# Layer two keeps squared h in SBUF, splits x later, and issues its odd bf16 products in eight tiles

## The chip, the cores and the metric

One core of a Trainium2 chip runs the whole program. The metric is device time in microseconds (us) of that core, as the median of several executions. The core's engines appear under these names: PE is TensorE (matmul), PEld its weight loads, DVE is VectorE, ACT is ScalarE, POOL is GpSimd, and SP is the queue from which all transfers are issued.

## The reference

```python
def _attn_ref(q, k, v) -> np.ndarray:
    B, H, S, D = q.shape
    factor = 4
    ...
    q_d = q.reshape(B, H, Sd, factor, D).mean(axis=3)
    ...
    out_up = np.repeat(out_d, factor, axis=2)
    pos = np.arange(S)
    mask = np.abs(pos[:, None] - pos[None, :]) < factor
    scores = scale * np.matmul(q, k.transpose(0, 1, 3, 2))
    scores = np.where(mask, scores, -1000000000.0)
    ...
    return (out_up + out_local).astype(np.float32)

def _moe_ref(x, w_in, w_out) -> np.ndarray:
    h = x @ w_in
    r = np.maximum(h, 0.0)
    g = r * r
    return (g @ w_out).astype(np.float32)
...
    x = np.ascontiguousarray(attn_out.transpose(0, 2, 1, 3)).reshape(B * S, H * D)
    x = _moe_ref(x=x, **moe_kwargs)
    return _moe2_ref(x=x, **moe2_kwargs)
```

q, k and v have 4 batches of 8 heads, 576 positions and 64 columns, so x is 2304 tokens by 512; both layers go from 512 to 2048 columns and back, and `_moe2_ref` computes the same as `_moe_ref` with its own weights. All is fp32.

## The kernel before

**Tiling.** The 2304 tokens are nine tiles of 256. The loop of the matmuls goes over 18 tiles, `n` = 0 to 8 for layer one and 9 to 17 for layer two (`NT` = 9), and in each over eight blocks of 256 hidden columns, `p` = 0 to 7. One pair (n, p) is a step. Attention and the conversion of the weights run between the steps of layer one.

**Precision by parts.** Each fp32 operand is kept as a high part (rounded by an fp32r cast) and a low part (operand minus high part), and a product of two operands is three products: high by high, high by low, low by high. x is split by `split_x` (line 841): two ACT casts of 512 columns give `xH`, two subtractions give `xL`, on DVE or POOL, whichever is planned to be free earlier (`either`, line 385). `fetch` (line 832) loads the x of a layer-two tile; `make_room` leaves one buffer `xr` for it.

**A step of layer two.** `mm_h` (line 863) makes h in one PSUM bank with 24 products of 256 columns. `act_h` (line 884) then works on ACT: Relu and Square in place in PSUM, a copy of the 128 columns a21 into the tile `S`, the cast of h to the high part of g, and, when the sums in `S` are there, their cast `SH`. `low_g` (line 909) works on DVE: four sums of 128 columns (the operand sums of a seven-product block scheme of Strassen's kind), the low part of g (h minus its high part), and the low part of the sums, `gSL`. `mm_y2` (line 936) issues 21 products: 12 that use the sums and 9 that use g alone. So a step is 45 products, against 48 in layer one, and PE runs h(i+1) between h(i) and y(i). In the first step of a tile (`p` = 0) the nine products on g come first, since the others wait until the tile before has left its accumulators.

**The end of a tile.** `leave` (line 1033) copies one quarter from PSUM on ACT and makes seven sums of 256 columns on DVE (line 1066) into a staging tile `ld[0]` or `ld[1]`, which is then stored.

**From layer one to layer two.** `quarters` (line 777) prepares differences of the second layer's output weights. `reload` (line 809) loads each 1024-column weight again from DRAM when layer one has done with it, rounds it on ACT and makes its low part on DVE or POOL. The last reloads, of `p` = 6 and 7, run beside the first steps of tile 9.

**The order.** Every chain above is a generator, and `Order.run` (line 136) is a list scheduler: at each turn it takes the operation that could start earliest by a model of durations, and writes the engines' queues in that order. An engine runs its queue strictly in order. A kind `DVP` in this plan is a DVE operation that also reserves the port which POOL shares with DVE (`PORT`, line 125).

**Odd products.** For steps listed in `KICK` (line 47), `mm_h` first issues one 128-column bf16 product of two identity matrices into the h bank (line 870); the next product overwrites it.

Of the kernel before, what the change touches and what calls it, by code (L numbers as in the profile page):

```python
# [8 lines left out]
F32 = mybir.dt.float32  # L9
# [13 lines left out]
NT = B * S // TN  # L23
# [20 lines left out]
NEAR = 0.02  # L44
FG = 0.4
FT = 3
KICK = {(n, 1) for n in (10, 12, 14)}
CL, GL, HL = 4, 4, 6
CP, CD, GP, UP = -0.848, 0.436, -1.416, -1.019
QP, VP, HP = -0.537, 0.649, -0.76  # L50
# [9 lines left out]
class Order:  # L60
# [75 lines left out]
    def run(self):  # L136
        while True:
            self.poll()
            best = None
            for th in self.live:  # L140
                if th.wish is not None and not callable(th.wish):
                    some = th.wish if isinstance(th.wish, list) else [th.wish]
                    _, t, eng, dur, *rows = min((self.start(th, w[0]) + w[1] * BIAS.get(w[0], 1.0), self.start(th, w[0]), *w) for w in some)
                    key = t
                    if best is None or key < best[0] - NEAR:
                        best = key, t, th, eng, dur, rows
            if best is None:
                assert not self.live, "nothing can start"
                return
            _, t, th, eng, dur, rows = best  # L150
            if eng in ("DVP", "POOL"):
                self.free["PORT"] = t + dur
            eng = "DVE" if eng == "DVP" else eng
            self.eng = eng
            if eng == "PE":
                if self.fill:
                    now = max(self.free.get("PE", 0.0), FT)
                    while now + FG < t:
                        now = self.stream(now, 0.22, 1.0)
                        self.fill()  # L160
                dur = self.stream(t, dur, *rows) - t
            if eng == "SP":
                self.free[eng] = t + (rows[0] if rows else 0.46)
                self.free["DMA"] = max(t + 1.1, self.free.get("DMA", 0.0)) + dur
                value = self.free["DMA"] + 2.0
            else:
                self.free[eng] = t + dur
                value = t + dur + LATENCY[eng]
            th.last, th.done = eng, value - LATENCY[eng]
            self.resume(th, value)  # L170
# [46 lines left out]
def attention_two_mlp_kernel(  # L217
# [151 lines left out]
    def dve(cols):  # L369
        return "DVE", 0.065 + cols / 957.0  # L370
# [11 lines left out]
    def act(cols):  # L382
        return "ACT", 0.065 + cols / 1150.0

    def either(cols):
        return [dvp(cols), pool(cols)]
# [390 lines left out]
    def quarters():  # L777
        yield lambda: ev.get("room")
        for p in range(NP):
# [19 lines left out]
            f_ld.put(n, tt)  # L799
            ev["T", p] = tt  # L800

    def quarter(p, name, low):
        if name in ("T3", "T4", "T2"):
            w, c = place[p, low][("T3", "T4", "T2").index(name)]
            return w[:, c:c + 256]
        m = ("B11", "T1", "B21", "B22").index(name)
        return weight(p, 1, low, 2)[:, m // 2, m % 2 * 256:m % 2 * 256 + 256]

    def reload(p, kind):
        yield o.at("scr", p, kind)  # L810
        if kind == 0:
            yield o.at("h", NT - 1, p)
        else:
            yield o.at("y", NT - 1, p)

        hi = weight(p, kind, 0, 2).rearrange("p k f -> p (k f)")
        some = pieces(p, kind, 1, 2, 0, 1024)
        for lo, c, n1 in some:
            yield dma(128 * 4 * n1, 4096 if n1 == 1024 else 2048)
            nc.sync.dma_start(out=lo.bitcast(F32), in_=wscr[p][kind][:, c:c + n1])  # L820
        for lo, c, n1 in some:
            yield act(n1)
            evac(hi[:, c:c + n1], lo.bitcast(F32))
        for lo, c, n1 in some:
            tt = yield either(n1)
            engine().tensor_tensor(out=lo, in0=lo.bitcast(F32), in1=hi[:, c:c + n1].bitcast(F32), op=ALU.subtract)
        count(("w", 2, p), 2, tt)

# [12 lines left out]
    def split_x():  # L841
        for n, (layer, t) in enumerate(seq):
            yield o.at("x", n)
            if n >= NXL:
                yield o.at("h", n - NXL, NP - 1)
            i = x_buf[n]
            for c in range(2):
                ks = slice(2 * c, 2 * c + 2)
                yield act(512)
                evac(xH[n % NXL][:, ks], xr[i][:, ks])  # L850
            for c in range(2):
                ks = slice(2 * c, 2 * c + 2)
                tt = yield either(512)
                engine().tensor_tensor(  # L854
                    out=xL[n % NXL][:, ks], in0=xr[i][:, ks], in1=xH[n % NXL][:, ks].bitcast(F32), op=ALU.subtract
                )
            f_xr.put(i, tt)
            ev["split", n] = tt
# [25 lines left out]
    def act_h():  # L884
        for i, st in enumerate(steps):
            yield o.at("h", *st)
            h = hb[i % 2]
            yield act(512)
            nc.scalar.activation(out=h, in_=h, func=AF.Relu)  # L889
            yield act(512)  # L890
            nc.scalar.activation(out=h, in_=h, func=AF.Square)  # L891
            if seq[st[0]][0] == 2:
                yield lambda: ev.get("room")
                if seq[steps[i - 1][0]][0] == 2:
                    yield o.at("gl", i - 1)
                if i == last:
                    yield o.at("y", *steps[i - 2])
                ev["sq", i] = yield act(128)
                nc.scalar.copy(late2["S"][:, 0:128], h[:, 128:256])
            ev["gh", i] = yield act(512)  # L900
            nc.scalar.copy(g_of(i, 0), h)  # L901
            if seq[st[0]][0] == 2:
                yield o.at("S", i)
                if seq[steps[i - 1][0]][0] == 2:
                    yield o.at("yS", i - 1)
                ev["gsh", i] = yield act(512)
                nc.scalar.copy(late2["SH"], late2["S"])  # L907

    def low_g():
        for i, st in enumerate(steps):  # L910
            two = seq[st[0]][0] == 2
            h = hb[i % 2]
            if two:


                yield o.at("sq", i)
                a11, _, a12, a22 = (h[:, 128 * m:128 * m + 128] for m in range(4))
                s1, s2, s3, s4 = (late2["S"][:, 128 * m:128 * m + 128] for m in range(4))
                for dst, a, b, op in (
                    (s3, a11, s1, ALU.subtract), (s1, s1, a22, ALU.add), (s2, s1, a11, ALU.subtract),  # L920
                    (s4, a12, s2, ALU.subtract),
                ):
                    tt = yield dve(128)
                    nc.vector.tensor_tensor(out=dst, in0=a, in1=b, op=op)  # L924
                ev["S", i] = tt
            yield o.at("gh", i)
            tt = yield dve(512)
            nc.vector.tensor_tensor(out=g_of(i, 1), in0=h, in1=g_of(i, 0).bitcast(F32), op=ALU.subtract)  # L928
            ev["gla", i] = tt
            if two:  # L930
                yield o.at("gsh", i)
# [238 lines left out]
```

## Time and profile before

| | us |
|---|---|
| median of 3 runs | 916.38 |
| lowest and highest run | 911.27, 916.97 |
| the profiled execution | 915.1 |
| its span, first to last instruction | 913.3 |
| mean granted TensorE clock, share of full speed | 0.988 |

The profile is that of one execution; its span leaves out 1.8 us of the time. A PE that is shown busy is not PE at its peak, since matmuls overlap: a stretch is best judged by the distance between the starts of equal work, such as one step to the next. Idle time is put down to the instruction that released the engine.

### The profile page before, as it was taken

The page shows a single profiled execution, that of the slowest core. Times are in us where ns is not written, and L with a number is a line of the kernel's source. Part 1 is how long each engine was busy: PE and PEld are TensorE (multiplying, and loading weights), DVE is VectorE, ACT ScalarE, POOL GpSimd, SP SyncE. Part 2 cuts the span into 40 slices and gives each one's busy share as a digit, 9 for nine tenths or more (in the row PEclk, how much of TensorE's full clock was granted, in tenths as well). Part 3 has the DMA queues.
Part 4 walks back from the last instruction along what each step waited for, and adds up shares of the span by engine and source line. Part 5 has one row for each costly group of instructions (what it writes and reads, how often), then busy time and mean ns, then how long its engine had stood idle before and what let it go on. Part 6 is the DMA issues. An engine that isn't in the chain of part 4 may idle for free.

```text
span 913.3 us, 20806 instructions
## 1 busy us (share of the span) xinstructions
PE 894.6 (98%) x8696; PEld 859.1 (94%) x8696; DVE 496.0 (54%) x1016; ACT 524.6 (57%) x1030; POOL 72.6 (8%) x78
## 2 busy tenths in 40 slices
PE   9989999999999999999999999999999999999996
PEld 5579999999999999999999989999999999999996
DVE  5696863575873534233324564655555564645454
ACT  3798974565577665543436655455545455545443
POOL 4211200020300000000001010000000000000000
PEclk9789999999999999999999999999999999999999
DMA  9999921363466676321216520101011010100000
GB/s 182 243 238 243 217 67 38 110 163 74 115 191 210 191 235 207 129 82 36 84 43 214 193 92 2 47 2 47 2 47 48 1 48 1 47 1 24 1 24 24
DMA packets 92430, 90.48 MB, mean 99 GB/s; under 512 B 62256, under 2 KB 68272, under 8 KB 92336
## 3 DMA queue, kind: packets, MB, share of 16 engines
q1 hardware_dynamic: 92336, 89.15, 35.6%
q8 instruction: 68, 1.11, 0.5%
q14 instruction: 26, 0.21, 0.1%
HBM read 70.25 MB, written 18.87 MB: 98 GB/s over the span
## 4 chain that ended last, share of the span: by engine, by line
PE 83%; DVE 5%; DMA 4%; ACT 4%; issue 1%; SPq 1%; POOL 0%; ACTq 0%; POOLq 0%
PE h L877 39%; PE y L961 18%; PE at L944 12%; PE y L944 4%; PE at L961 3%; DMA s<-in_moe_w_out_dram 2%; DVE S L924 1%; PE at L452 1%; DVE ld L1066 1%; DMA ld<-in_v_dram 1%; PE at L643 1%; DMA s<-in_moe_w_in_dram 1%; DVE xL L854 1%; PE at L588 1%; PE at L478 1%
## 5 line engine op out<-in xcount | busy, mean ns | idle before, releaser
L877 PE MATMUL h<-xH,w 128*128 128x256 f32 x2304 | 317.2, 281 | 1.7 <-ACT xH L392 1.7
L877 PEld LDWEIGHTS h<-xH,w 128*128 128x128 f32 x2304 | 287.4, 189 | 4.2 <-ACT xH L392 1.8
L961 PE MATMUL y<-g,w 128*128 128x256 f32 x1536 | 191.0, 279 | 0.7 <-ACT g L901 0.6
L889 ACT ACTIVATE h<-h 128x512 f32<-128x512 f32 x144 | 84.0, 583 | 179.2 <-PE h L877 179.0
L961 PEld LDWEIGHTS y<-g,w 128*128 128x128 f32 x1536 | 180.7, 188 | 3.6 <-ACT g L901 1.8
L877 PE MATMUL h<-xL,w 128*128 128x256 f32 x1152 | 180.4, 279 | 2.1 <-DVE xL L854 2.1
L928 DVE TENSOR_TENSOR g<-h,g 128x512 fp32r<-128x512 f32 x144 | 98.6, 685 | 115.7 <-ACT g L901 113.5
L877 PEld LDWEIGHTS h<-xL,w 128*128 128x128 f32 x1152 | 154.3, 189 | 2.6 <-DVE xL L854 2.6
L924 DVE TENSOR_TENSOR S<-h,S 128x128 f32<-128x128 f32 x144 | 41.9, 291 | 158.0 <-ACT g L901 152.8
L907 ACT CAST SH<-S 128x512 fp32r<-128x512 f32 x72 | 44.8, 622 | 97.4 <-DVE S L924 93.8
L891 ACT ACTIVATE h<-h 128x512 f32<-128x512 f32 x144 | 84.2, 585 | 3.4
L901 ACT CAST g<-h 128x512 fp32r<-128x512 f32 x144 | 84.9, 589 | 1.4
L854 POOL TENSOR_TENSOR xL<-xr,xH 128x512 fp32r<-128x512 f32 x14 | 19.7, 1405 | 478.7 <-ACT xH L392 478.7
L933 DVE TENSOR_TENSOR gSL<-S,SH 128x512 fp32r<-128x512 f32 x72 | 51.1, 710 | 10.0 <-ACT SH L907 1.1
L944 PE MATMUL at<-w,SH 128*128 128x256 f32 x224 | 45.4, 284 | 1.9 <-ACT SH L907 1.9
L924 DVE TENSOR_TENSOR S<-S,h 128x128 f32<-128x128 f32 x144 | 41.4, 288 | 5.6 <-ACT g L901 0.8
L944 PEld LDWEIGHTS at<-w,SH 128*128 128x128 f32 x224 | 34.1, 189 | 3.3 <-ACT SH L907 2.7
L944 PE MATMUL at<-w,g 128*128 128x256 f32 x240 | 35.0, 282 | 0.4 <-DVE g L928 0.4
L944 PE MATMUL at<-w,gSL 128*128 128x256 f32 x112 | 32.4, 289 | 1.4 <-DVE gSL L933 1.3
L944 PEld LDWEIGHTS at<-w,g 128*128 128x128 f32 x240 | 31.3, 192 | 0.6 <-DVE g L928 0.6
L459 DVE TENSOR_REDUCE qkd<-at 128x256 f32<-128x1024 f32 (+1 forms) x19 | 20.9, 1108 | 12.6 <-ACT qkT L392 12.5
L392 ACT ACTIVATE qkT<-at 128x1024 f32<-128x1024 f32 (+1 forms) x19 | 17.8, 936 | 16.9 <-PE at L452 16.7
(248 smaller groups left out, 1207.8 us busy)
## 6 DMA issues: line engine op xcount, KB each, us to landing
s<-in_moe_w_in_dram SPq DMA_DIRECT2D x32, 256.0 KB
s<-in_moe_w_out_dram SPq DMA_DIRECT2D x16, 512.0 KB
ws<-ga SPq DMA_DIRECT2D x32, 256.0 KB
w<-ws SPq DMA_DIRECT2D x13, 512.0 KB
ld<-in_moe_w_in_dram SPq DMA_DIRECT2D x12, 512.0 KB
ld<-in_moe_w_out_dram SPq DMA_DIRECT2D x10, 512.0 KB
xr<-ys SPq DMA_DIRECT2D x9, 512.0 KB
vw<-in_v_dram SPq DMA_DIRECT2D x68, 64.0 KB
```

The lines of the kernel that those rows point to most:

```text
L459: nc.vector.tensor_reduce(out=qkd[:, :, :, 32 * c:32 * c + n // 4], in_=got.rearrange("p z m (g r) -> p z m g r", r=4), op=ALU.add, axis=AX.X,
L854: engine().tensor_tensor(out=xL[n % NXL][:, ks], in0=xr[i][:, ks], in1=xH[n % NXL][:, ks].bitcast(F32), op=ALU.subtract)
L877: nc.tensor.matmul(out=o, lhsT=wt[p, 0][:, 1084:1340][:, fs] if w is wL and kk == 0 and p in ODD else w[:, kk, fs], rhs=x[:, kk], start=(i ...
L889: nc.scalar.activation(out=h, in_=h, func=AF.Relu)
L891: nc.scalar.activation(out=h, in_=h, func=AF.Square)
L901: nc.scalar.copy(g_of(i, 0), h)
L907: nc.scalar.copy(late2["SH"], late2["S"])
L924: nc.vector.tensor_tensor(out=dst, in0=a, in1=b, op=op)
L928: nc.vector.tensor_tensor(out=g_of(i, 1), in0=h, in1=g_of(i, 0).bitcast(F32), op=ALU.subtract)
L933: nc.vector.tensor_tensor(out=late2["SL"], in0=late2["S"], in1=late2["SH"].bitcast(F32), op=ALU.subtract)
L944: nc.tensor.matmul(out=seven(n, m - 1), lhsT=lhsT, rhs=quarter(p, w, low), start=p == 0 and x == 0 and m not in (2, 3, 6), stop=p == NP - ...
L961: nc.tensor.matmul(out=yb[e // 2][:, (e % 2) * 256:(e % 2) * 256 + 256], lhsT=w[:, fi, e * 128:e * 128 + 128], rhs=g[:, fi * 256:fi * 256 ...
```

## The change

- **h squared goes to SBUF.** The staging tile `ld[1]` is given up after the last `quarters` and serves as two halves of 512 columns, `late2["G"]`. In layer two, Relu reads PSUM and writes G, Square works in place in G, and the cast to g, the four sums and the low part of g read G. The copy of a21 into `S` is gone, and so is the wait for the step before that it had. The sums and the low part are planned as `DVP`.
- **The next tile's x.** In layer two both `xL` subtractions are on DVE. From the first step of layer two on, the scheduler adds 1.2 us to the key of a `split_x` operation, so that one is chosen only where nothing else can start within 1.2 us.
- **Reload.** The weights of `p` = 6 and 7 come in pieces of 256 columns (16 in place of 5 pieces), with their low parts on DVE alone.
- **Odd products.** They stand in the fourth step of the eight tiles 10 to 17, where they stood in the second step of tiles 10, 12 and 14.

```diff
 NEAR = 0.02
 FG = 0.4
 FT = 3
-KICK = {(n, 1) for n in (10, 12, 14)}
+LAZY = dict(split_x=1.2)
+FINE, HALF = 6, 1
+KICK = {(n, 3) for n in range(10, 18)}
 CL, GL, HL = 4, 4, 6
 CP, CD, GP, UP = -0.848, 0.436, -1.416, -1.019
 QP, VP, HP = -0.537, 0.649, -0.76
...
                 if th.wish is not None and not callable(th.wish):
                     some = th.wish if isinstance(th.wish, list) else [th.wish]
                     _, t, eng, dur, *rows = min((self.start(th, w[0]) + w[1] * BIAS.get(w[0], 1.0), self.start(th, w[0]), *w) for w in some)
-                    key = t
+
+                    key = t + (LAZY.get(th.gen.__name__, 0.0) if ("h", NT, 0) in self.ev else 0.0)
                     if best is None or key < best[0] - NEAR:
                         best = key, t, th, eng, dur, rows
             if best is None:
...
             f_ld.put(n, tt)
             ev["T", p] = tt
 
+        yield from f_ld.give_up([1])
+        late2["G"] = [ld[1].bitcast(F32)[:, 512 * m:512 * m + 512] for m in range(2)]
+        ev["G"] = 0.0
+
     def quarter(p, name, low):
         if name in ("T3", "T4", "T2"):
             w, c = place[p, low][("T3", "T4", "T2").index(name)]
...
 
         hi = weight(p, kind, 0, 2).rearrange("p k f -> p (k f)")
         some = pieces(p, kind, 1, 2, 0, 1024)
+        if p >= FINE:
+            some = [(x[:, u:u + 256 * HALF], c + u, 256 * HALF) for x, c, n1 in some for u in range(0, n1, 256 * HALF)]
         for lo, c, n1 in some:
             yield dma(128 * 4 * n1, 4096 if n1 == 1024 else 2048)
             nc.sync.dma_start(out=lo.bitcast(F32), in_=wscr[p][kind][:, c:c + n1])
...
             yield act(n1)
             evac(hi[:, c:c + n1], lo.bitcast(F32))
         for lo, c, n1 in some:
-            tt = yield either(n1)
+            tt = yield either(n1) if p < FINE else dvp(n1)
             engine().tensor_tensor(out=lo, in0=lo.bitcast(F32), in1=hi[:, c:c + n1].bitcast(F32), op=ALU.subtract)
         count(("w", 2, p), 2, tt)
 
...
                 evac(xH[n % NXL][:, ks], xr[i][:, ks])
             for c in range(2):
                 ks = slice(2 * c, 2 * c + 2)
-                tt = yield either(512)
+                tt = yield either(512) if layer == 1 else dvp(512)
                 engine().tensor_tensor(
                     out=xL[n % NXL][:, ks], in0=xr[i][:, ks], in1=xH[n % NXL][:, ks].bitcast(F32), op=ALU.subtract
                 )
...
         for i, st in enumerate(steps):
             yield o.at("h", *st)
             h = hb[i % 2]
-            yield act(512)
-            nc.scalar.activation(out=h, in_=h, func=AF.Relu)
-            yield act(512)
-            nc.scalar.activation(out=h, in_=h, func=AF.Square)
-            if seq[st[0]][0] == 2:
-                yield lambda: ev.get("room")
-                if seq[steps[i - 1][0]][0] == 2:
-                    yield o.at("gl", i - 1)
+            two = seq[st[0]][0] == 2
+            if two:
+                yield lambda: ev.get("G")
                 if i == last:
                     yield o.at("y", *steps[i - 2])
-                ev["sq", i] = yield act(128)
-                nc.scalar.copy(late2["S"][:, 0:128], h[:, 128:256])
+            g = late2["G"][i % 2] if two else h
+            ev["relu", i] = yield act(512)
+            nc.scalar.activation(out=g, in_=h, func=AF.Relu)
+            ev["sq", i] = yield act(512)
+            nc.scalar.activation(out=g, in_=g, func=AF.Square)
             ev["gh", i] = yield act(512)
-            nc.scalar.copy(g_of(i, 0), h)
+            nc.scalar.copy(g_of(i, 0), g)
             if seq[st[0]][0] == 2:
                 yield o.at("S", i)
                 if seq[steps[i - 1][0]][0] == 2:
...
 
 
                 yield o.at("sq", i)
-                a11, _, a12, a22 = (h[:, 128 * m:128 * m + 128] for m in range(4))
+                a11, a21, a12, a22 = (late2["G"][i % 2][:, 128 * m:128 * m + 128] for m in range(4))
                 s1, s2, s3, s4 = (late2["S"][:, 128 * m:128 * m + 128] for m in range(4))
                 for dst, a, b, op in (
-                    (s3, a11, s1, ALU.subtract), (s1, s1, a22, ALU.add), (s2, s1, a11, ALU.subtract),
+                    (s3, a11, a21, ALU.subtract), (s1, a21, a22, ALU.add), (s2, s1, a11, ALU.subtract),
                     (s4, a12, s2, ALU.subtract),
                 ):
-                    tt = yield dve(128)
+                    tt = yield dvp(128)
                     nc.vector.tensor_tensor(out=dst, in0=a, in1=b, op=op)
                 ev["S", i] = tt
             yield o.at("gh", i)
-            tt = yield dve(512)
-            nc.vector.tensor_tensor(out=g_of(i, 1), in0=h, in1=g_of(i, 0).bitcast(F32), op=ALU.subtract)
+            g = late2["G"][i % 2] if two else h
+            tt = yield dvp(512) if two else dve(512)
+            nc.vector.tensor_tensor(out=g_of(i, 1), in0=g, in1=g_of(i, 0).bitcast(F32), op=ALU.subtract)
             ev["gla", i] = tt
             if two:
                 yield o.at("gsh", i)
```

## Rows read from the trace of the kernel before

**Rows 1.** The page: PE's busy time and share; granted clock in 40 equal slices.
```profile
PE 894.6 (98%) x8696; PEld 859.1 (94%) x8696; DVE 496.0 (54%) x1016; ACT 524.6 (57%) x1030; POOL 72.6 (8%) x78
PEclk9789999999999999999999999999999999999999
```

**Rows 2.** Chain that ended last, 570 to 700: start, length, engine, tile, line, products.
```profile
582.05 2.83 PE h L877 x24
...
650.95 2.83 PE h L877 x24
653.78 2.47 PE at L944 x21
656.33 2.79 PE h L877 x24
...
661.49 2.72 PE h L877 x24
...
671.89 2.72 PE h L877 x24
...
687.22 2.72 PE h L877 x24
```

**Rows 3.** Timeline of PE (start, length, instruction): first and last products of layer two.
```profile
519.84 0.40 PE L877 MATMUL h<-xH,w 128*128 128x256 f32 x2
...
906.46 0.28 PE L944 MATMUL at<-w,gSL 128*128 128x256 f32 x1
```

**Rows 4.** Timeline of PE, h(9,2) to h(9,3); in brackets idle time and releaser.
```profile
530.40 0.28 PE L877 MATMUL h<-xH,w 128*128 128x256 f32 x1
...
535.16 0.51 PE L944 MATMUL at<-w,SH 128*128 128x256 f32 x2 [1.88 <-ACT SH L907]
...
539.76 0.51 PE L877 MATMUL h<-xH,w 128*128 128x256 f32 x3
```

**Rows 5.** Busy time of a stretch; last three: granted clock, DMA share, GB/s.
```profile
519.84:541.00 21.16, 19.06 (x151) 18.66 (x150) 14.50 (x26) 13.51 (x25) 2.41 (x1) 0.92 0.43 150
```

**Rows 6.** Timelines of ACT and DVE in the same stretch.
```profile
534.49 0.62 ACT L907 CAST SH<-S 128x512 fp32r<-128x512 f32 x1 [2.07 <-DVE S L924]
...
532.66 1.22 DVE L826 TENSOR_TENSOR w<-w 128x1024 fp32r<-128x1024 f32 x1
```

**Rows 7.** Timeline of PE, tile borders, first and last of six.
```profile
573.32 0.84 PE L944 MATMUL y<-w,g 128*128 128x256 f32 x6
...
581.89 0.28 PE L877 MATMUL h<-xH,w 128*128 128x256 f32 x1
...
825.83 0.28 PE L944 MATMUL y<-w,g 128*128 128x256 f32 x1
...
834.40 0.28 PE L877 MATMUL h<-xH,w 128*128 128x256 f32 x1
```

**Rows 8.** Timelines of POOL and DVE at the border of tiles 13 and 14.
```profile
743.45 1.30 POOL L854 TENSOR_TENSOR xL<-xr,xH 128x512 fp32r<-128x512 f32 x1 [40.76 <-ACT xH L392]
...
743.50 1.79 DVE L854 TENSOR_TENSOR xL<-xr,xH 128x512 fp32r<-128x512 f32 x1
```

**Rows 9.** Timelines of ACT and DVE, an ordinary step.
```profile
711.45 0.58 ACT L889 ACTIVATE h<-h 128x512 f32<-128x512 f32 x1 [1.77 <-PE h L877]
...
713.47 0.29 DVE L924 TENSOR_TENSOR S<-h,S 128x128 f32<-128x128 f32 x1 [3.07 <-ACT g L901]
...
715.47 0.69 DVE L933 TENSOR_TENSOR gSL<-S,SH 128x512 fp32r<-128x512 f32 x1
```

**Rows 10.** Groups by line and shape: count, busy us, mean ns of one, idle before.
```profile
L907 ACT CAST SH<-S 128x512 fp32r<-128x512 f32 x69 | 42.9, 622 | 93.5 <-DVE S L924 91.4 <-PE at L944 2.1
...
L1041 ACT COPY ld<-y 128x512 f32<-128x512 f32 x4 | 2.1, 586 | 2.7 <-PE y L961 2.7
...
L392 ACT ACTIVATE w<-w 128x256 fp32r<-128x256 f32 x3 | 1.2, 407 | 0.0
```

**Rows 11.** One line's instructions (last of `quarters`): shortest/median/longest ns, first and last start.
```profile
L796 DVE TENSOR_TENSOR q_hd<-ld,q_hd x1: 421/421/421, 496.5 to 496.5; 128x256 fp32r<-128x256 f32 x1
```

## The prediction

> **What bounds it now.** I read the page first. PE is busy for 98% of the span and its clock is granted in full except in the first slices and around the change of layers [rows 1]. So what can be won is time in which PE waits, or in which its products stand further apart than they could. The change touches layer two and the last reloads before it, so layer two is what I take apart, by the chain of waits and PE's timeline.
>
> The chain shows two distances. A step (45 products) takes 15.33 / 3 = 5.11 us in the stretch from 671.89, but 68.90 / 13 = 5.30 us from 582.05 [rows 2]. The engine is as busy in both, and the clock is granted in full in both slices. So the same products run at 113.6 or at 117.8 ns each, and a spacing once entered lasts. A slow step costs 0.19 us.
>
> The products of layer two start at 519.84 and the last one starts at 906.46 [rows 3], 386.6 us later. At the fast distance, 72 steps and the last y block of layer one, which stands among them (24 products, 2.7), would need 368.0 + 2.7 = 370.7 us. The excess is 16.0 us (rounded), and the timeline of PE divides it:
>
> - The change of layers: from 530.40 to 539.76 PE makes one step in 9.36 us, 4.25 too many [rows 4].
> - Six of the eight tile borders: y, h, y (66 products, 7.5 us when fast) take 8.57 us at the first and at the last of them [rows 7]; the six lose between 0.2 and 1.1 us each, 5.3 in all.
> - Slow distance behind two of these borders: from 582.05 until the odd product ahead of 656.33 [rows 2], 14 steps, and from 834.40 [rows 7] through the last h, some 12 steps: 26 x 0.19 = 5.0.
> - Three odd products. The h block behind one starts 0.08 us late (653.78 + 2.47 = 656.25, and it starts at 656.33), and the step that it opens takes 5.16 in place of 5.11 [rows 2]: 0.13 each, 0.4.
> - What is left, 1.05, lies in the last three y blocks.
>
> **The change, part by part.**
>
> *h squared in SBUF.* In an ordinary step Relu starts at 711.45, the first sum on DVE at 713.47, and gSL ends at 715.47 + 0.69 = 716.16: 4.71 us [rows 9]. PE needs it one step after h, 5.11, so there are only some tenths of slack. The first sum reads h and the copied a21, both long there, yet the row puts its wait on the cast of g, which also only reads h. That cast stands in the way of the sums. The Trainium skill has a reason (PSUM — Partial Sum Buffer, section on bank collisions): no two engines may access one PSUM bank at once, two reads included, so software keeps them apart. The trace agrees: 2.02 us from Relu to the first sum. After the change the bank is read by Relu alone, and the sums need only Square. Relu from PSUM to SBUF I take as the copy of y, 586 ns, Square and the cast from SBUF to SBUF as the cast SH, 622 ns [rows 10]. The first sum then starts 0.59 + 0.62 + 0.07 (two hand-overs) = 1.28 after Relu, 0.74 earlier; four sums and SH follow unchanged, and gSL ends about 4.0 after Relu, 0.7 earlier. The sums and the low part with both inputs in SBUF I price as now; gSL, 0.69, has such inputs already. If the sums still stand behind the cast, the first one starts at 1.28 + 0.62 = 1.9 and the gain is 0.1: these are the two ends, and I take 0.7, because of the named releaser.
>
> A rule of the skill speaks against this part (VectorE: DVE Perf Modes, the section on the TRN2 errata): a ScalarE operation costs 224 cycles beside its columns from SBUF, 172 from PSUM. That is 43 ns more each, an estimate from that page; the rows have 622 against 586, 36 ns. By the page the chain would gain 0.73 in place of 0.74.
>
> On ACT the copy goes and two operations grow by 36 ns: less work, none of it on the path, since ACT idles 1.77 us ahead of Relu [rows 9]. The new wait for G holds Relu of (9,0) and all of ACT's queue behind it, but ld[1] is free once the last quarters are done, shortly after 496.5 [rows 11], while h(9,0) starts at 519.84 [rows 3]: nothing. The staging of tiles has one buffer left and a whole tile (41 us) to empty it: nothing. That h's bank is free earlier gains nothing: its next user starts 7.5 us after.
>
> *x later, and not on POOL.* At a border the xL half on DVE takes 1.79 us where POOL started the other half 0.05 earlier; an operation of that form alone takes 0.69 [rows 8, 9]. It stands ahead of the border step's sums in DVE's queue, beside the seven sums of `leave`, and PE then waits for SH and gSL. DVE alone needs 2 x 0.69 per tile, and the 1.2 us rule puts both subtractions into the pause ahead of the first sum (3.07 us [rows 9]) and both casts into ACT's 1.77. Moved past them are the border step's sums, gSL and `leave`, which all come earlier; the fetch of the next x, behind the split, has the rest of the tile. Without the 1.1 us of blocking and 0.7 of a subtraction, and with the chain 0.7 shorter, a border that is late by about 0.9 has slack. I take 5.3 -> 0.4; the ends are 0 and 5.3.
>
> *Reload in pieces.* At 532.66 a piece of 1.22 us stands between the sums on DVE; SH ends at 535.11 [rows 6], 2.0 after h(9,2) has ended (530.40 + 2.72). A piece of 256 costs 0.42 on DVE [rows 11] and 0.41 on ACT [rows 10]. So each place where a piece gets into the chain costs 0.8 less on DVE, the chain itself is 0.7 shorter, and x is not split there. That removes the 2.0, or leaves some tenths where several small pieces get in. The rest of the 4.25 is mostly clock: it is granted at 0.92 in this stretch [rows 5], and a short wait should leave it alone, as the borders' do. I take 4.25 -> 1.0; ends 0 and 4.25. The eleven further transfers stand on SP ahead of nothing that is due soon: these weights are needed some 20 us later.
>
> *Odd products.* The three seen left PE fast; one of them found it slow, at 656 [rows 2]. They stood ahead of the border's waits, behind which PE turned slow. In the fourth step they stand after them, so that the wide spacing lasts three steps of a tile (0.6) instead of tiles. Cost 8 x 0.13 = 1.0. Slow distance 5.0 -> 0.9 (three steps behind two or three borders, and part of tile 9, which has no odd product); ends 0 and 6.8 (below).
>
> *The tail.* The last chain is 0.7 shorter, and the last y's waits shrink: 1.05 -> 0.55.
>
> Sum of the excess after: 1.0 + 0.4 + 0.9 + 1.0 + 0.55 = 3.9, so 12.1 us of 16.0 go. The profiled execution took 915.1 us (span 913.3, 1.8 around it): 915.1 - 12.1 = 903.0. The median of the runs is 916.38, 1.3 above the profiled one, and one run was at 911.27, perhaps with less slow distance.
>
> **Rivals.**
>
> A, the forecast: 903.0, from 899.5 (no excess but the odd products: 915.1 - 15.0 = 900.1, less half a microsecond of scatter) to 906.5 (the change of layers keeps its 4.25).
>
> B, the odd products don't bring PE back; 656 was chance. For it: two of the three found PE fast already, and PE also turned fast after some borders without one. Against it: at 656 the next products are fast at once. Half of the 72 steps slow is 6.8 in place of 0.9: 908.9.
>
> C, the sums stay behind the cast in SBUF too, because the wait follows the tile and not the bank. The chain gains 0.1; borders keep 1.5, the change of layers 2.5, slow steps 1.5: 903.0 + 1.1 + 1.5 + 0.6 = 906.2. Against it: the cast and the sums only read.
>
> D, the borders stay late, because the seven sums of `leave`, not x, are ahead of the chain. Then 4.9 of the borders' 5.3 come back and 1.0 of slow steps: 908.9. Against it: at two borders PE loses nothing, though the seven sums are there.
>
> E, slower: x comes too late. If the rule never finds its gap, the split is planned when all else is blocked, and each tile's first h waits for two casts and two subtractions, 2 x 0.62 + 2 x 0.69 = 2.6 us, eight times 21: 924. It decides once no pause of over 1.2 us is left on ACT or DVE in eight steps; the idle times of 1.77 and 3.07 [rows 9] speak against it.
>
> **How the numbers follow.** A 0.55, B 0.15, C 0.12, D 0.10, E 0.08. The time is A's. The range, 899.5 to 911, holds A and C, and B and D with two microseconds above them, and leaves out E and a tenth of the rest. Within 1% of 916.38, about what a measurement of this kernel can tell from no change, begins at 907.2: A and half of C are faster (0.61), B, D and the other half of C the same (0.31), E slower (0.08).
>
> **What would show it.** In the profile after: the first sum some 1.3 us behind Relu, not 2.0; no POOL work after the reloads; borders of 7.5 us; no granted clock under 1 at the change of layers; steps of 5.11 from every fourth step of a tile on. I am wrong if steps of 5.30 stand behind an odd product, if PE waits for xL at a tile's first h, or if SH is still 2 us late in tile 9.

## The result, and the profile after

| | before | after |
|---|---|---|
| median of 19 runs, us | 915.44 | 907.24 |
| lowest and highest run, us | 908.77, 917.44 | 904.98, 912.61 |
| the profiled execution, its span, us | 915.1, 913.3 | 912.6, 910.8 |
| layer two, first to last product, us | 386.6 | 378.1 |

The ratio is 0.9917, with a 95% interval of 0.9903 to 0.9930: 0.8% faster, 8.2 us by the medians. The forecast was 903.0, so the time is 4 us above it, though inside the range, and the gain stays within 1%.

The profiled execution of after is the slowest of its runs: in its first 100 us, in code that the change leaves alone, PE waits 4.0 us for one DVE result and the clock is granted at 0.86 in the stretch from 75 to 100. It enters layer two at 525.69 in place of 519.84. What follows compares layer two from its first to its last product, where the profiles differ by 8.5 us and the medians by 8.2.

The page of after, to be read against [rows 1]:

```profile
PE 888.7 (98%) x8701; PEld 857.3 (94%) x8701; DVE 488.4 (54%) x1035; ACT 520.6 (57%) x969; POOL 61.9 (7%) x70
PEclk9989899999999999999999999999999999999999
```

PE's share of busy time is the same 98%: the page alone doesn't show what changed. Of the groups by line and shape, three that are new (count, busy us, mean ns of one, idle before and its releaser):

```profile
L931 DVE TENSOR_TENSOR S<-ld 128x128 f32<-128x128 f32 x144 | 35.7, 289 | 153.2 <-ACT ld L906 153.2
L906 ACT ACTIVATE ld<-ld 128x512 f32<-128x512 f32 x72 | 45.5, 631 | 2.3
L908 ACT CAST g<-ld 128x512 fp32r<-128x512 f32 x72 | 44.8, 622 | 2.3
```

The first sums (L931) now wait for Square (L906), no longer for the cast to g, as in [rows 9]. The timelines of ACT and DVE at the border of tiles 13 and 14 show it in one step:

```profile
742.02 0.60 ACT L904 ACTIVATE ld<-h 128x512 f32<-128x512 f32 x1 [1.83 <-PE h L886]
742.65 0.63 ACT L906 ACTIVATE ld<-ld 128x512 f32<-128x512 f32 x1
743.32 0.62 ACT L908 CAST g<-ld 128x512 fp32r<-128x512 f32 x1
...
743.32 0.49 DVE L931 TENSOR_TENSOR S<-ld 128x128 f32<-128x128 f32 x2 [0.17 <-ACT ld L906]
...
745.21 0.69 DVE L941 TENSOR_TENSOR gSL<-S,SH 128x512 fp32r<-128x512 f32 x1
```

The first sum starts 743.32 - 742.02 = 1.30 us after Relu, in the same instant as the cast that reads the same tile, and gSL ends 745.21 + 0.69 - 742.02 = 3.88 after it. Before it was 2.02 and 4.71 [rows 9]. These steps are typical: the medians of all 72 are 1.29 and 3.88 in after, 2.02 and 4.71 in before. Not all of the 0.72 comes from the cast that the sums no longer stand behind: the copy of a21, which is gone too, held its place on ACT for 0.16 us (in the step of [rows 9] it starts at 712.68 and the cast at 712.84). POOL has no work left in layer two, and in all of layer two the waits view lists no wait of PE, and one of its weight loads, 0.3 us.

The change of layers, by the busy time of the stretch (columns as in [rows 5]): PE has no gap, and the clock is granted in full, where it was 0.92.

```profile
525.70:542.00 16.30, 16.30 (x146) 16.30 (x145) 11.37 (x31) 13.09 (x31) 0.00 (x0) 1.00 0.50 164
```

So all waits are gone. What is left is spacing, in the chain that ended last (start, length, h blocks only; columns as in [rows 2]):

```profile
582.47 2.88 PE h L886 x24
...
619.63 2.83 PE h L886 x24
...
625.00 2.80 PE h L886 x24
...
630.18 2.72 PE h L886 x24
...
666.01 2.88 PE h L886 x24
```

The block at 582.47 stands behind the odd product of the step (10, 3). PE was at the close spacing before it (5.11 us per step) and is at the wide one after it (5.30). Eight steps later, behind the odd product of (11, 3), the h block is 2.72 long again; at (12, 3), 666.01, it turns wide once more. This goes on to the end: wide from the fourth step of tiles 10, 12, 14 and 16 to the fourth step of the next tile, 32 steps in all, 32 x 0.19 = 6.1 us. Over 370.7 us, layer two has an excess of 378.1 - 370.7 = 7.4: 6.1 of wide spacing, 8 x 0.13 = 1.0 of the odd products themselves (from 625.00 to 666.01 are 41.01 us, 0.13 more than eight steps of 5.11), and 0.3 of the rest.

### The profile page after: what moved, and what is told of

It reads as the page before. It is cut to its first block, busy times and chain, and to the rows that moved or that the text cites. A ratio compares the mean times of both kernels' runs of the same rounds, so it can differ in the third digit from the quotient of the medians.

```text
span 910.8 us, 20739 instructions
## 1 busy us (share of the span) xinstructions
PE 888.7 (98%) x8701; PEld 857.3 (94%) x8701; DVE 488.4 (54%) x1035; ACT 520.6 (57%) x969; POOL 61.9 (7%) x70
## 4 chain that ended last, share of the span: by engine, by line
PE 89%; DMA 6%; SPq 2%; DVE 1%; ACT 1%; issue 0%; ACTq 0%
PE h L886 42%; PE y L969 19%; PE at L952 14%; PE y L952 5%; DMA ld<-in_v_dram 3%; PE at L969 2%; DMA s<-in_moe_w_out_dram 2%; DMA s<-in_moe_w_in_dram 2%; PE at L455 1%; SPq L442 1%; PE at L646 1%; PE at L591 1%; PE at L481 1%; PE at L521 1%; PE at L628 1%; PE at L511 1%
## 5 line engine op out<-in xcount | busy, mean ns | idle before, releaser
L904 ACT ACTIVATE ld<-h 128x512 f32<-128x512 f32 x72 | 43.1, 598 | 133.1 <-PE h L886 133.1
L931 DVE TENSOR_TENSOR S<-ld 128x128 f32<-128x128 f32 x144 | 35.7, 289 | 153.2 <-ACT ld L906 153.2
L936 DVE TENSOR_TENSOR g<-h,g 128x512 fp32r<-128x512 f32 x72 | 49.6, 689 | 117.0 <-ACT g L908 116.6
L904 ACT ACTIVATE h<-h 128x512 f32<-128x512 f32 x72 | 42.0, 583 | 97.8 <-PE h L886 97.6
L936 DVE TENSOR_TENSOR g<-ld,g 128x512 fp32r<-128x512 f32 x72 | 49.2, 684 | 0.1
L906 ACT ACTIVATE ld<-ld 128x512 f32<-128x512 f32 x72 | 45.5, 631 | 2.3
L908 ACT CAST g<-ld 128x512 fp32r<-128x512 f32 x72 | 44.8, 622 | 2.3
L906 ACT ACTIVATE h<-h 128x512 f32<-128x512 f32 x72 | 42.2, 586 | 1.3
L908 ACT CAST g<-h 128x512 fp32r<-128x512 f32 x72 | 42.0, 584 | 1.4
```

Of the source, the lines that this page charges most:

```text
L904: nc.scalar.activation(out=g, in_=h, func=AF.Relu)
L906: nc.scalar.activation(out=g, in_=g, func=AF.Square)
L908: nc.scalar.copy(g_of(i, 0), g)
L936: nc.vector.tensor_tensor(out=g_of(i, 1), in0=g, in1=g_of(i, 0).bitcast(F32), op=ALU.subtract)
```

## The experiments

Each kernel was compared with the kernel before on the same chip. They ran in three groups: p_none to p_mixed (median of before 914.52), p_piece and u_g to u_fine (915.26), and g_only to u_g_third (912.87). Ratios are to be compared across groups, not times. Where "one run" is said, the time is that of the profiled run alone. Each layer-two time is that of one profiled run.

### Are the odd products to blame? (p_none)

The changed kernel without them.

```diff
-KICK = {(n, 3) for n in range(10, 18)}
+KICK = set()
```

> The changed kernel without any odd product. Flip theory (each odd product turns PE from one spacing to the other): all 72 steps of layer two at 5.11 us, layer two from first to last product 370.7 + 0.5 = 371 us against 378.1, so about 7 us less than the changed kernel, some 900 us. Rival, alternation by tile (every other tile is slow by its accumulators or its x, whatever the odd products do): the slow tiles stay, 377 us, some 906 us. Rival of the prediction (an odd product brings PE back to the close spacing): without them nothing brings it back, so at least as many slow steps as now, 377 us or more.

Measured: 899.15 us, ratio 0.9838 (0.9814 to 0.9862). All 72 steps are close, and layer two takes 371.0 us in place of 378.1 (timeline of PE of p_none, first and last products of layer two):

```profile
519.33 0.63 PE L886 MATMUL h<-xH,w 128*128 128x256 f32 x4
...
890.37 0.28 PE L952 MATMUL at<-w,gSL 128*128 128x256 f32 x1
```

So nothing in the rest of the change needs an odd product, and the eight of them cost 7.1 us. In after, the prediction's "bring PE back" had nothing to bring back; instead they sent PE off.

### One, and none behind it (p_one)

```diff
-KICK = {(n, 3) for n in range(10, 18)}
+KICK = {(10, 3)}
```

> One odd product only, in the fourth step of tile 10. Flip theory: 5.11 us before it and 5.30 in all 61 steps behind it up to the end, 61 x 0.19 = 11.6 us more than without one, layer two 383 us. Alternation by tile: as without one. Prediction's theory (it brings PE back): no slow step behind it.

Measured (one run): 911.21 us, layer two 382.5. All steps are close up to (10, 3) and all 61 from there on are wide: 371.0 + 61 x 0.19 = 382.6. The chain of p_one, the h block behind the odd product and one near the end:

```profile
576.70 2.88 PE h L886 x24
...
884.16 2.83 PE h L886 x24
```

One odd product turns a close PE wide, and nothing in 61 steps turns it back. Two readings of the alternation in after remain: any odd product flips the state, or the place decides.

### Flip, or place? (p_second, p_mixed)

Eight odd products in the second step of a tile, where three had stood before; and seven in seven different steps.

```diff
-KICK = {(n, 3) for n in range(10, 18)}
+KICK = {(n, 1) for n in range(10, 18)}
```

> Odd products in the second step of the tiles 10 to 17, not in the fourth. Flip theory: slow and fast in turn from second step to second step, layer two 378 us. If the place in the tile decides (before the change the three odd products of second steps left PE at the close spacing each time): all at 5.11, layer two 370.7 + 0.5 + 8 x 0.14 = 372.3 us.

Measured (one run): 899.47 us, layer two 372.3. All eight found PE close and left it close, for 372.3 - 371.0 = 1.3, or 0.16 each. The chain of p_second, the h block behind the first of them and the next:

```profile
564.99 2.80 PE h L886 x24
...
570.17 2.72 PE h L886 x24
```

The flip falls: the place decides.

```diff
-KICK = {(n, 3) for n in range(10, 18)}
+KICK = {(10, 0), (11, 2), (12, 4), (13, 5), (14, 6), (15, 7), (17, 1)}
```

> Seven odd products, in the first step of tile 10, third of 11, fifth of 12, sixth of 13, seventh of 14, eighth of 15 and second of 17. Flip theory: each of the seven changes the spacing, fast to slow at the first, slow to fast at the next, and so on. If the place decides, some of them don't.

Measured (one run): 902.83 us, layer two 375.5. The chain of p_mixed, the h block behind an odd product and the one after it:

```profile
560.03 2.88 PE h L886 x24
...
565.39 2.83 PE h L886 x24
...
613.16 2.79 PE h L886 x24
...
618.33 2.75 PE h L886 x24
...
664.41 2.80 PE h L886 x24
...
669.59 2.72 PE h L886 x24
...
756.67 2.88 PE h L886 x24
...
762.03 2.83 PE h L886 x24
```

(10, 0) at 560.03 and (14, 6) at 756.67 turn a close PE wide; (12, 4) at 664.41, and likewise (13, 5) and (17, 1), leave it close; (11, 2) at 613.16, and likewise (15, 7), find it wide and make it close. Taken with after, the steps seen so far to turn a close PE wide are those with `p` = 0, 3 and 6. These three are a set that the kernel has by name (`ODD`): for these blocks the first low piece of the input weight lies 4 columns, 16 bytes, ahead of its regular place, and it is loaded by the second product behind the odd one.

### Is it the shifted piece? (p_piece)

In (10, 3) the second product behind the odd one, and its like in the block's second half, reads the regular piece next to it in place of the shifted one; in (12, 1), where no shift is, it reads 4 columns ahead. Otherwise as p_none, with six odd products:

```diff
-KICK = {(n, 3) for n in range(10, 18)}
+KICK = {(10, 3), (12, 1), (13, 1), (14, 1), (15, 3), (16, 1)}
...
+    def low0(n, p, fs):
+        if (n, p) == (10, 3):
+            return weight(p, 0, 1)[:, 1, fs]
+        if (n, p) == (12, 1):
+            return wt[p, 0][:, 1020:1276][:, fs]
+        return wt[p, 0][:, 1084:1340][:, fs] if p in ODD else weight(p, 0, 1)[:, 0, fs]
...
-                out=o, lhsT=wt[p, 0][:, 1084:1340][:, fs] if w is wL and kk == 0 and p in ODD else w[:, kk, fs],
+                out=o, lhsT=low0(n, p, fs) if w is wL and kk == 0 else w[:, kk, fs],
```

> Where does an odd product turn PE to the wide spacing? So far in steps of p = 0, 3 and 6, not in p = 1, 4, 5. The weights of p = 0, 3, 6 lie 64 columns further apart, and their first low piece, which the second product behind the odd one loads, starts 4 columns (16 bytes) ahead of that. Odd products in (10,3), (12,1), (13,1), (14,1), (15,3), (16,1). In step (10,3) the second product loads another low piece (of the next 128 rows of the contraction) in place of the shifted one; in step (12,1) it loads the low piece from 4 columns ahead (both change the numbers of the output, not the count or size of the products). If the shifted piece decides: (10,3) stays close, (12,1) turns wide, (13,1) turns back, (14,1) stays close, (15,3) turns wide, (16,1) back; layer two some 374 us. If the layout of p as a whole decides: (10,3) turns wide and (12,1) turns back to close; (15,3) wide, (16,1) back.

Measured (one run): 902.34 us, layer two 374.3. The chain of p_piece (in this kernel L893 is the h block; those at 575.99, 647.67 and 690.20 stand right behind an odd product):

```profile
575.99 2.80 PE h L893 x24
...
581.17 2.72 PE h L893 x24
...
647.67 2.88 PE h L893 x24
...
653.03 2.83 PE h L893 x24
...
690.20 2.79 PE h L893 x24
...
695.37 2.72 PE h L893 x24
```

(10, 3), which turned PE wide in after and in p_one, leaves it close without the shift, and (12, 1), harmless in p_second, turns it wide with one; (13, 1) at 690.20 brings it back. (14, 1), (15, 3) and (16, 1) also do what was expected of them if the piece decides. So the place acts through this one piece, not through the layout of `p`. The products of (10, 3) and (12, 1) part at the seventh behind the odd one (113 against 118 ns), before the second half, from the 13th on, loads its own. The swap changes the values that are loaded along with their address; no run separates the two. Taken together: an odd product that finds PE wide makes it close, with the shift (after, at (11, 3)) or without it; one that finds PE close leaves it so, unless the second product behind it loads a piece 16 bytes off the regular place. Without an odd product the same shifted pieces are loaded in every tile and change nothing (p_none).

### What does each other part do? (u_g, u_x, u_fine)

All three without odd products, so beside p_none. u_g puts h squared back into PSUM, and keeps x and the reload as changed:

```diff
+            nc.scalar.activation(out=h, in_=h, func=AF.Relu)
...
+            nc.scalar.activation(out=h, in_=h, func=AF.Square)
...
-            nc.scalar.activation(out=g, in_=h, func=AF.Relu)
...
-            nc.scalar.activation(out=g, in_=g, func=AF.Square)
...
+                nc.scalar.copy(late2["S"][:, 0:128], h[:, 128:256])
...
-            nc.scalar.copy(g_of(i, 0), g)
+            nc.scalar.copy(g_of(i, 0), h)
```

> The changed kernel without odd products, and with h squared in PSUM as before (copy of a21, sums and low part of g from the bank); x, reload as changed. Theory of the prediction: the chain from Relu to gSL is 4.7 us again, with some tenths of slack, so tile borders wait a few tenths for SH or gSL even without x, the change of layers keeps about 1.5 us of its 4.25, and a wait may leave PE at the wide spacing: layer two 374 to 378 us against 371.0, some 903 to 907 us. Rival (x on POOL at the border was the whole of it): layer two 371 to 372 us, 899 to 900 us.

Measured: 911.63 us (ten runs from 905.72 to 915.00), ratio 0.9949 (0.9923 to 0.9975), layer two 384.0: the expected 374 to 378 was missed. The waits shrink as expected: the change of layers has 0.5 left and the first border 0.26 in its y block. But from that first border to the end PE runs wide. Where the 0.15 us stall at this border comes from can be read off PE's weight loads and DVE's sums of `leave` in u_g:

```profile
569.01 0.41 PEld L954 LDWEIGHTS y<-q_qkT,g 128*128 128x128 f32 x3
569.57 0.30 PEld L954 LDWEIGHTS at<-w,SH 128*128 128x128 f32 x2 [0.15 <-issue]
...
569.04 0.42 DVE L1076 TENSOR_TENSOR ld<-ld,at 128x256 f32<-128x256 f32 x1
```

SH and gSL of this step had ended long before (567.47 and 568.68), so they aren't it. The sum at 569.04 is the fourth of the seven, on which the code lets the next tile into its accumulators (`left3`); it ends at 569.46, and PE goes on 0.11 later. In before the fourth sum of the first border ends at 574.18 and PE's load starts at 574.30, 0.12 later; in after it ends at 575.10, and the load, due at 575.67, goes on without a stall. At all eight borders of b_none and of u_g_third (both below) the load starts 0.12 after the fourth sum too. So the border's first stall is PE waiting for `leave`; gSL, which is ahead of the third and later sums in DVE's queue, ends earlier with the shorter chain, and the sums with it.

u_x splits x as before (no extra 1.2, either engine):

```diff
-LAZY = dict(split_x=1.2)
+LAZY = {}
...
-                tt = yield either(512) if layer == 1 else dvp(512)
+                tt = yield either(512)
```

> The changed kernel without odd products, and with the split of x as before (no 1.2 us on its key, xL on DVE or POOL); h squared in SBUF and reload as changed. Theory of the prediction: where POOL starts first, DVE is held up for 1.1 us at the border; the chain is 0.7 us shorter, so some borders stay late by up to 0.5 us, 2 us in all, and PE may turn to the wide spacing behind them: layer two 372 to 377 us. Rival (the shorter chain alone clears the borders): layer two 371 to 371.5 us, 899 us.

Measured: 900.16 us, ratio 0.9841 (0.9821 to 0.9860), layer two 371.7. No border waits. The one wait is at the change of layers (timeline of PE of u_x):

```profile
531.94 0.39 PE L952 MATMUL at<-w,SH 128*128 128x256 f32 x2
532.81 0.38 PE L952 MATMUL at<-w,gSL 128*128 128x256 f32 x1 [0.48 <-DVE gSL L941]
```

u_fine reloads in pieces as before:

```diff
-FINE, HALF = 6, 1
+FINE, HALF = 8, 1
```

> The changed kernel without odd products, and with the reload as before (whole weights, low parts on DVE or POOL); h squared in SBUF and x as changed. Theory of the prediction: pieces of 1.2 us stand in the chain of the first steps of tile 9, so PE waits some 1 us there and the clock may fall for a while: layer two 372 to 374 us. Rival (the shorter chain alone clears the change of layers): layer two 371 us.

Measured: 897.89 us, ratio 0.9812 (0.9798 to 0.9827), layer two 370.9, no wait of PE. Where the chain is short, the finer pieces are not needed, and at the borders the later x isn't either (u_x); at the change of layers it saves u_x's wait. This is the fastest version that was run; its layer two is that of p_none within 0.1 us, so the pieces are not shown to cost anything there.

### The first part alone (g_only), and before without its odd products (b_none)

g_only is the kernel before with h squared in SBUF and no odd product: x split and reload as before.

```diff
-KICK = {(n, 1) for n in (10, 12, 14)}
+LAZY = {}
+FINE, HALF = 8, 1
+KICK = set()
...
+            nc.scalar.activation(out=g, in_=h, func=AF.Relu)
...
+            nc.scalar.activation(out=g, in_=g, func=AF.Square)
```

> The kernel before with h squared in SBUF alone: x and reload as before, no odd product. If the shorter chain is the gain: borders clear, all steps at 5.11 but for some tenths to 3 us at the change of layers (there x, whole pieces of reload and POOL come together), layer two 371 to 374 us, 898 to 902 us. If x or the reload carry a share that the shorter chain hides only together with them: waits at the borders, then wide spacing, over 905 us.

Measured: 899.71 us, ratio 0.9871 (0.9844 to 0.9898), layer two 372.2. The borders are clear. At the change of layers PE waits for gSL (timeline of PE of g_only):

```profile
532.35 0.39 PE L952 MATMUL at<-w,SH 128*128 128x256 f32 x2
533.72 0.38 PE L952 MATMUL at<-w,gSL 128*128 128x256 f32 x1 [0.97 <-DVE gSL L941]
```

Its chain has, between the sums and the low part of g, a reload piece:

```profile
531.24 1.22 DVE w L835
532.45 0.60 DVE g L936
533.06 0.61 DVE gSL L941
```

This y block is 3.64 long in place of 2.38, 1.26 too many: the piece of 1.22 us stands ahead of gSL on DVE. With both the late x and the pieces undone it costs 1.3, with x alone 0.8 (u_x), with the pieces alone nothing (u_fine). One part of four, without odd products, gives 1.3%; the whole change gave 0.8%.

b_none is the kernel before without its three odd products.

```diff
-KICK = {(n, 1) for n in (10, 12, 14)}
+KICK = set()
```

> The kernel before without its three odd products. If a wait at a border turns PE to the wide spacing and nothing turns it back: wide from the first or second border to the end, but no waits at the borders behind that (the wide spacing gives them slack): up to 64 x 0.19 = 12.2 us in place of 5.0, waits 1 to 2 us in place of 5.3, some 916 to 919 us. If the odd products of before did nothing: as before, 915 us.

Measured: 911.67 us, ratio 1.0002 (0.9981 to 1.0022). The expectation fell: PE did not stay wide to the end. In its profile seven borders lose about 1.0 us each, in two stalls of some 0.25 and 0.75; the eighth, behind which there is no x left to split, has only the first. Timelines of PE's loads and of PE and DVE, border of tiles 11 and 12:

```profile
660.72 0.30 PEld L944 LDWEIGHTS at<-w,SH 128*128 128x128 f32 x2
...
662.24 1.10 PE L877 MATMUL h<-xH,w 128*128 128x256 f32 x8
...
663.65 1.10 PE L877 MATMUL h<-xH,w 128*128 128x256 f32 x8
...
665.81 0.39 PE L944 MATMUL at<-w,gSL 128*128 128x256 f32 x1 [0.23 <-DVE gSL L933]
...
661.18 1.64 DVE L854 TENSOR_TENSOR xL<-xr,xH 128x512 fp32r<-128x512 f32 x1
```

The first is the one of u_g (the fourth sum ends at 660.60, PE's load starts at 660.72). Here it turns PE wide: the 12 products from 662.24 to 663.65 take 1.41 us, 117.5 ns each. The second stall, a step later, is the wait for gSL behind x's subtraction of 1.64, and PE is close again after it. But this is the one border of eight where the first stall leaves PE wide. At the others PE is back at the close spacing within the same y block, as at the border of tiles 10 and 11, where the same 12 products take 1.35:

```profile
620.32 1.07 PE L877 MATMUL h<-xH,w 128*128 128x256 f32 x8
...
621.67 1.07 PE L877 MATMUL h<-xH,w 128*128 128x256 f32 x8
```

So a border's stall can turn PE wide, and need not. In the profile of before the first stall left PE wide at four of five borders (first steps of tiles 10, 13, 14 and 15, not 16); the second stall made it close again at 13, 14 and 15, left it wide at 10, and at 16 turned a close PE wide. There a second wait often did what the odd products were meant to do, and by the medians the three of them changed nothing that can be measured.

### An odd product where it is wanted (u_g_third)

u_g, with odd products in the third step of a tile, whose pieces are at their regular place and which follows the border's stall.

```diff
-KICK = set()
+KICK = {(n, 2) for n in range(10, 18)}
```

> The kernel with h squared in PSUM, x and reload as changed, and an odd product in the third step (p = 2, where no shifted low piece is loaded) of the tiles 10 to 17. If an odd product in such a step always leaves PE at the close spacing: each tile is close from its third step on, wide for one or two steps behind a border's wait at most; the waits at the borders (some 0.3 to 0.9 us) come back in every tile, since a close-spaced tile leaves less slack. Layer two 373 to 377 us, some 903 to 906 us against 911.6 without odd products. If it only turns the spacing over: wide and close in turn, 909 us or more.

Measured: 903.41 us (four runs from 902.00 to 904.26), ratio 0.9898 (0.9872 to 0.9924); layer two 375.2 in place of u_g's 384.0. Chain of u_g_third, the y blocks at and behind the border of tiles 10 and 11:

```profile
610.98 2.63 PE at L954 x21
...
616.48 2.38 PE at L954 x21
```

The block of 2.63 holds the stall; the next one, behind the odd product, is at 2.38. But the odd product isn't what brought PE back here. Timelines of PE at the first border, behind the stall, in u_g (first two lines) and in u_g_third:

```profile
569.91 0.28 PE L954 MATMUL at<-w,gSL 128*128 128x256 f32 x1
...
571.09 0.52 PE L886 MATMUL h<-xH,w 128*128 128x256 f32 x3
...
571.03 0.28 PE L954 MATMUL at<-w,gSL 128*128 128x256 f32 x1
...
572.17 0.23 PE L879 MATMUL h<-ident 128*128 128x128 bf16 x1
```

The ten products from the first gSL product on take 1.18 us in u_g, 118 ns each, and 1.14 in u_g_third, 114 each, although the two kernels issue the same products up to there. At all eight borders of u_g_third the last products before the odd one are 113 or 114 ns apart. So in this profile the eight odd products found PE close and left it close. The ratio, 0.9898 against u_g's 0.9949, fits an odd product that catches PE where a stall has turned it wide, as (11, 2) of p_mixed did in the same step of a tile; this profile holds no such case, so that is not shown here.

## Why the prediction came out as it did

**The chain through SBUF: right.** 1.30 and 3.88 us after Relu, where 1.28 and 4.0 were forecast; rival C, the sums still behind the cast, falls with the two starts at 743.32. The rule of the Trainium skill (PSUM — Partial Sum Buffer, bank collisions) that two readers of a bank are kept apart agrees: 2.02 us with the bank, 1.30 without; no run separates the bank from an order that the software sets for it. The other rule of the Trainium skill cited (VectorE: DVE Perf Modes, TRN2 errata, 43 ns more from SBUF by an estimate from that page) agrees too: the cast takes 622 ns against 584, Square 631 against 586, for the same operations on PSUM in layer one of after. The longer Square stands in the chain, but no wait of PE came of it.

**The change of layers: right in direction, 1.0 forecast, 0 measured.** The pieces were credited with part of it; by u_fine the shorter chain and the late x do it without them. That the rest of the 4.25 was mostly clock is borne out: in the same step b_none waits as long for SH (1.9 us), its clock stays at 1.00, and it loses 2.65.

**The borders: right in size (0.4 forecast, 0 measured), incomplete in cause.** The forecast put the loss on x and POOL, and the cure on the later x, with 0.7 from the chain. The runs show two stalls. The second and larger is the one of the forecast, gSL behind x. The first, some 0.25 us a border, is PE waiting for `leave`'s fourth sum. Rival D also blamed these sums, but as standing ahead of the chain; here the chain's gSL stands ahead of them, so a shorter chain moves them, which D's price of 4.9 leaves out. The later x removes the second stall alone (u_g_third: the first stall at all eight borders, no wait for gSL there). The shorter chain removes both without the later x (u_x, g_only).

**The odd products' own cost: right.** 0.13 each in after, as forecast; 0.16 in p_second.

**"In the fourth step ... the wide spacing lasts three steps of a tile": the step that failed.** 0.9 us of wide spacing were forecast and 6.1 measured. In after no stall is left at the borders, so there was nothing to bring back. The inference rested on one odd product that found PE wide (656.33 in [rows 2]) and two that left it close, all in the second step of a tile, and carried them over to the fourth as if the step didn't matter. In the fourth step the shifted piece makes an odd product turn a close PE wide. The excess is rival B's (6.8 for half of the steps), but not for B's reason: an odd product does bring a wide PE back, four times in after. The words that I would be wrong "if steps of 5.30 stand behind an odd product" named the sign.

**The tail:** p_none's excess over 370.7 is 0.3, with no wide step and no odd product, where 0.55 was forecast.

**The sum.** 12.1 us were forecast to go, 8.5 went: 5.2 less by the wide spacing, and 1.0, 0.4 and 0.25 more by the change of layers, the borders and the tail. Without the odd products the changed kernel is at 0.9838 of before, 0.8% under its own time. The median of 907.24 lies above the forecast's own end of 906.5; it is inside the range because that was drawn up to 911 for rivals B and D, and neither of their mechanisms was at work. That is luck.

**Open:** why the two spacings exist; why a stall of 0.07 to 0.15 us at a border leaves PE wide in one case and not in the next (6 of the 22 first stalls in the profiles of before, b_none, u_g and u_g_third), and why a later wait often undoes it; through what the shifted piece acts. p_one, p_second, p_mixed and p_piece were run once each; p_one holds one case of the rule, the others six to eight. One profile doesn't tell how long a kernel with stalls is usually wide: by their profiles b_none's layer two is 381.6 and that of before 386.6, yet the medians agree, and u_g's ten runs differ by 9.3 us.

## What to carry to other kernels

Move an operand that two engines want to read at the same time out of its PSUM bank: here this one edit, with the copy that it makes needless, shortened the chain by 0.8 us per step, cleared all borders, and was worth more alone, without odd products, than the whole change. An edit that repairs the consequences of a wait has to be measured again, and in its new place, once the wait is gone. Judge PE by the distance of equal steps and not by its busy share, which is 98% with the waits and without.

## What the hardware showed that was not expected

- At a clock granted in full, the same stream of products runs at 113.6 or 117.8 ns each, and stays there: for 61 steps, 323 us, in p_one.
- The state can be switched by one bf16 product of 128 columns, which costs 0.13 to 0.16 us. All nine that found PE wide made it close (after, p_mixed, p_piece, before); of those that found it close, the ones with a piece of weights 16 bytes off its regular place at the second product behind them turned it wide, and no other did.
- A stall of 0.15 us cost some 12 us in u_g: behind its first border 62 steps run at 5.30 in place of 5.11. In u_g_third eight such stalls cost no wide step.
